# A fused attention and feed-forward kernel: transposes of the next chunk moved two pairs later, six q/k products gathered at the phase change, output products spread 2, 4, 5, 5

## The chip, the cores and the metric

The kernel runs on one core of one Trainium2 chip. The metric is the device time of one execution in microseconds (us), the median of several runs. The profile comes from one further execution of the same program, and its times are counted from that execution's first instruction.

## What is computed

The input x has 2048 rows of 448 numbers in bfloat16. Each row is normalized. From the normalized rows come a sliding-window attention (16 heads of width 28, each row attends to itself and the 7 rows at distances 2, 4, ..., 14 before it) and a feed-forward of width 1792. The output joins the two:

```python
xn = _layernorm(x)
qkv = xn @ wqkv                                   # 16 heads of 28
idx = pos[:, None] - (arange(8) * 2)[None, :]     # dilated window
attn = softmax(where(idx >= 0, einsum(q, k[idx]) * 28 ** -0.5, -1e9))
s = einsum(attn, v[idx]) @ wo
h = gelu(xn @ w1 + b1)
g = silu(h @ w2 + b2)
out = x + s * g
```

## The kernel before

Even rows are processed before odd rows, so that the dilated window is a plain one. The 2048 rows are 16 tiles of 128 rows, in four chunks of four tiles. Everything is kept in SBUF.

**Order of the work.** The instructions of TensorE (PE), ScalarE (ACT), VectorE (DVE) and GpSimd stand on each engine in the order in which the code issues them (`tc.manual_schedule`, L382). Instructions issued before L382 (memsets, DMAs) are placed by the scheduler.

**Start (L383 to L428).** Eight dummy matmuls (`busy`), then for tiles 0 to 3: statistics (`ln_stats`), the reciprocal deviation on ACT (`ln_rstd`), the normalization on DVE (`ln_apply`), four 128x128 transposes on PE (`ln_tr`) and a copy into the transposed array xnT (`ln_put`). Between them stand the first v products (`v_mm`). Then DVE spreads the q/k weights from the staging tile wraw to wqk (L182), and PE makes the q and k products of chunk 0. In this document T2 and T3 are the transposes of tiles 2 and 3, v1, v2, v3 the v products that follow.

**Four rounds, c = 0 to 3.** Each has two phases.

- `feed_forward_1(c)`: seven pairs k = 0 to 6 of first feed-forward products for chunk c. A pair is two PSUM banks, six full matmuls (L224) and two half-height ones (L233), and its two gelu activations on ACT (L239). `ffn1_even` ends with the half-height ones, `ffn1_odd` begins with them. Pair 0 is made in the phase before. Between the pairs stand: the transposes of chunk c+1 (after k = 1 and k = 3), two q and two k products of chunk c+1 (after k = 5), the silu of chunk c-1 (tanh on ACT, L268, then g on DVE, L269), the row statistics of chunk c+2, and output products (`wo_job`: four matmuls L288, then sg and o_t on DVE, then a DMA out on SP's queue).
- The attention phase (c below 3): the q and k products of head group 2, then five units of 121 queries. A unit is S (16 small matmuls, L312), two exp on ACT (L317), two mask products on DVE (L319), AV (16 small matmuls into psO, L328), a shuffle of the denominators on DVE (L332), Ln and Exp on ACT (L335, L336) and the division into oT on DVE (L337). Beside each unit stands one second feed-forward product (`ffn2_job`, 14 matmuls L257, called y0 to y15 here, put into SBUF by DVE at L264). The fifth unit is followed by pair 0 of the next chunk.

**The tail.** Before `feed_forward_1(3)` all but the last two units are done. After it stand units 15 and 16, y12 to y15, and the output products 8 to 15 (wo8 to wo15).

**PSUM.** Eight banks in two pools. psA (tag A) has two buffers of two banks, used by S and by the pairs k = 1, 2, 4, 5. psB (tag B) has four buffers of one bank, used by all else: pT, q/k, v, y, wo, psO and the pairs k = 0, 3, 6. A new psB tile gets the buffer that is released first in the order of the code, and its first matmul waits for the last reader of the tile before it. So a transpose can wait for a division of an attention unit, and a feed-forward pair for the sg of an output product.

**Waits through SBUF.** wraw has 904 columns. The DMAs write columns 0 to 895, and a memset (L125) clears columns 896 to 903; the ranges interleave row by row, and the memset waits for both DMAs.

Of the kernel before, what the change touches and what calls it, by code (L numbers as in the profile page):

```python
# [10 lines left out]
U32 = mybir.dt.uint32  # L11
# [22 lines left out]
def kernel(  # L34
# [60 lines left out]

    nc.vector.memset(wz[:].bitcast(U32), 0)
# [28 lines left out]
    nc.vector.memset(wraw[:, :, 2 * D:2 * D + 8].bitcast(U32), 0)  # L125
# [49 lines left out]
    def ln_put(t, pT, copy):  # L175
        copy(xnT[:, :, LEAD + t * P:LEAD + (t + 1) * P], pT[:, :, :])  # L176
# [16 lines left out]
    def q_job(c, g):  # L193
        qk_job(c, g, 0, nc.vector.tensor_copy)
# [19 lines left out]
    def ffn1_tiles(k):  # L214
        if k % 3 == 0:
            return [psB.tile([P, CH], F32, name="ps_h", tag="B") for _ in range(2)]
        ps = psA.tile([P, 2, CH], F32, name="ps_h", tag="A")
        return [ps[:, i, :] for i in range(2)]
# [130 lines left out]
    def feed_forward_1(c, ps, wos):  # L349
# [4 lines left out]
        for k in range(0, MT // 2, 2):  # L354
# [6 lines left out]
            if c + 1 < NC and k < 4:  # L361
                for j in (k, k + 1):
                    ln_put(nx + j, ln_tr(nx + j), nc.vector.tensor_copy)
            if c and k < 4:
                silu_job(4 * (c - 1) + k)
                silu_job(4 * (c - 1) + k + 1)
            if c + 1 < NC and k == 4:
                for g in range(2):
                    q_job(c + 1, g)
                    k_job(c + 1, g, nc.vector.tensor_copy)  # L370
            if c + 2 < NC and 2 <= k < 6:
                ln_stats(nx + 4 + k - 2)
                ln_stats(nx + 4 + k - 1)
            for _ in range(2):
                if k >= 2 and wos:
                    wo_job(wos.pop(0))
# [5 lines left out]
    with tc.manual_schedule(engines={ENG.PE, ENG.Activation, ENG.DVE, ENG.Pool}):  # L382
# [47 lines left out]
        for c in range(3):  # L430
            feed_forward_1(c, ps, [0, 1, 2] if c == 2 else [])
# [6 lines left out]
            q_job(n, 2)  # L438
            k_job(n, 2)
# [18 lines left out]
        feed_forward_1(3, ps, [3, 4, 5, 6, 7])  # L458
        wo_job(8)
        E = qk_unit(15)  # L460
        ffn2_job(12)
        s9 = wo_mm(9)
        norm = av_unit(15, E)
        wo_put(9, s9)
        E = qk_unit(16)
        norm()
# [3 lines left out]
        s10 = wo_mm(10)  # L470
        norm = av_unit(16, E)
        norm()
        wo_put(10, s10)
        nc.scalar.preload_act_table_set(SET_GELU)
        s11 = wo_mm(11)
        y14 = ffn2_job(14, False)
        wo_put(11, s11)
        s12 = wo_mm(12)
        ffn2_put(14, y14)
        wo_put(12, s12)  # L480
        silu_job(13)
        silu_job(14)
        s13 = wo_mm(13)
        wo_put(13, s13)
# [36 lines left out]
```

## Time and profile before

| | |
|---|---|
| median of 3 runs | 184.22 us (183.9 to 184.52) |
| the profiled execution | 184.21 us, of which the span from first to last instruction is 182.6 us |
| PE busy | 165.5 us (91%) |
| ACT busy | 125.3 us (69%) |
| DVE busy | 118.0 us (65%) |
| TensorE clock, mean granted | 0.972 of full speed |
| output DMAs | 16 of 112.0 KB, on SP's queue |

A row of the time order reads: start, duration, engine, line, operation, output<-input, shape, xcount, and in square brackets how long the engine was idle before it and what ended that. Rows merge equal instructions that follow each other; the duration then runs from the first start to the last end. Matmuls overlap, so what a stretch costs on PE is read from start to start. Some matmul records are missing, so a count may be one short.

The first feed-forward phase of chunk 1 lies at 61 to 79 us, that of chunk 2 at 100 to 121 us, that of chunk 3 at 143 to 159 us.

### The profile page before, as it was taken

The numbers are of one execution on the slowest core, as the hardware profiler recorded it, in microseconds if no ns is written. First come the engines' busy times: TensorE is split into PE (matmuls) and PEld (weight loads), VectorE is DVE, ScalarE is ACT, GpSimd is POOL, SyncE is SP. The second block draws the span as 40 slices with busy tenths as digits, with TensorE's granted clock in tenths as the row PEclk, the third lists the DMA queues.
The fourth block names the chain that finished last, engine by engine and source line by source line (L and its number), as shares of the span: only waits on it lengthen the run. The fifth ranks groups of instructions, "written<-read, shape, count | busy, mean of one in ns | idle before, by whom it ended". The sixth has DMA issues, their size and how long they took to land.

```text
span 182.6 us, 3260 instructions
## 1 busy us (share of the span) xinstructions
PE 165.5 (91%) x1308; PEld 76.6 (42%) x1324; DVE 118.0 (65%) x266; ACT 125.3 (69%) x197; POOL 4.6 (2%) x16
## 2 busy tenths in 40 slices
PE   7489999999999789999999679999999999999870
PEld 2144444444555334444544334445455343355430
DVE  6563864456888436938886546728676425977793
ACT  3633297466888699396879796186788699767620
POOL 6020000000000000000000000000000000000000
PEclk9958999999999999999999999999999999999996
DMA  5999951000000000000000000000000000210021
GB/s 153 220 284 317 377 148 40 0 0 5 0 4 0 0 0 4 0 0 0 4 0 4 2 0 25 25 29 0 4 0 0 4 2 0 101 54 25 25 75 50
DMA packets 10990, 9.03 MB, mean 49 GB/s; under 512 B 2592, under 2 KB 10976, under 8 KB 10976
## 3 DMA queue, kind: packets, MB, share of 16 engines
q1 hardware_dynamic: 10688, 8.61, 15.8%
q10 hardware_dynamic: 288, 0.23, 0.4%
q8 instruction: 10, 0.16, 0.4%
q14 instruction: 4, 0.03, 0.1%
HBM read 7.00 MB, written 1.84 MB: 48 GB/s over the span
## 4 chain that ended last, share of the span: by engine, by line
PE 60%; ACT 24%; DVE 8%; DMA 3%; issue 2%; SPq 1%; DVEq 0%
PE ps_y L257 18%; PE ps_qk L188 12%; PE ps_h L224 11%; ACT E L317 6%; PE ps_v L203 5%; ACT hT L239 5%; PE ps_s L288 4%; DMA wraw<-in_A_wqkv_dram 3%; PE S L312 3%; ACT den L336 3%; PE ps_h L233 3%; ACT den L335 2%; PE psO L328 2%; DVE sg L294 2%; DVE g L269 2%
## 5 line engine op out<-in xcount | busy, mean ns | idle before, releaser
L239 ACT ACTIVATE hT<-ps_h,b1f 128x512 bf16<-128x512 f32 x56 | 34.4, 701 | 15.7 <-PE ps_h L233 14.9
L257 PE MATMUL ps_y<-w,hT 128*128 128x448 bf16 x224 | 45.1, 353 | 0.0
L224 PE MATMUL ps_h<-xnT,w 128*128 128x512 bf16 x160 | 40.4, 380 | 0.6 <-DVE sg L294 0.2
L317 ACT ACTIVATE E<-S 128x976 bf16<-128x976 f32 x34 | 32.0, 986 | 7.3 <-PE S L312 6.3
L188 PE MATMUL ps_qk<-xnT,wqk 128*128 128x512 bf16 x120 | 29.2, 379 | 0.4
L257 PEld LDWEIGHTS <-hT 128*128 128x128 bf16 x224 | 20.8, 98 | 19.3
L319 DVE TENSOR_TENSOR E<-E,mk_gen 128x976 bf16<-128x976 bf16 x30 | 19.8, 665 | 10.8 <-ACT E L317 10.8
L224 PEld LDWEIGHTS <-w 128*128 128x128 bf16 x168 | 15.2, 98 | 20.1 <-issue 4.8
L337 DVE TENSOR_TENSOR oT<-psO,den 128x484 bf16<-128x484 f32 (+1 forms) x17 | 11.2, 661 | 12.4 <-ACT den L336 12.4
L188 PEld LDWEIGHTS <-wqk 128*128 128x128 bf16 x128 | 12.3, 98 | 14.9 <-issue 1.1
L191 DVE CAST qT<-ps_qk 128x512 bf16<-128x512 f32 x16 | 11.0, 687 | 10.4 <-PE ps_qk L188 10.4
L269 DVE SCALAR_TENSOR_TENSOR g<-th,y 128x448 bf16<-128x448 bf16 x15 | 8.7, 621 | 13.7 <-ACT th L268 13.7
L203 PE MATMUL ps_v<-wv,xnT 128*128 128x448 bf16 x68 | 17.2, 392 | 0.0
L288 PE MATMUL ps_s<-wo,oT 128*128 128x448 bf16 x64 | 13.9, 353 | 1.5 <-DVE xnT L176 1.0
L335 ACT ACTIVATE den<-den 128x484 f32<-128x484 f32 (+1 forms) x17 | 10.4, 611 | 5.3 <-DVE den L332 5.3
L208 ACT CAST vw<-ps_v 128x448 bf16<-128x448 f32 x17 | 9.1, 536 | 6.0 <-PE ps_v L203 6.0
L172 PE MATMUL pT<-ident,xnb 128*128 128x128 bf16 x64 | 6.1, 232 | 6.9 <-DVE oT L337 3.4
L332 DVE STREAM_SHUFFLE den<-psO 128x484 f32<-128x484 f32 (+1 forms) x17 | 11.8, 695 | 0.0
L268 ACT ACTIVATE th<-y 128x448 bf16<-128x448 f32 x15 | 8.2, 601 | 4.3 <-DVE y L264 4.3
L336 ACT ACTIVATE den<-den 128x484 f32<-128x484 f32 (+1 forms) x17 | 10.3, 605 | 0.5
L233 PE MATMUL ps_h<-xnT,w 64*128 64x512 bf16 x56 | 9.9, 383 | 0.5 <-ACT hT L239 0.2
L294 DVE SCALAR_TENSOR_TENSOR sg<-ps_s,g 128x448 bf16<-128x448 f32 x16 | 9.9, 616 | 0.2
(60 smaller groups left out, 132.1 us busy)
## 6 DMA issues: line engine op xcount, KB each, us to landing
out_dram<-o_t SPq DMA_DIRECT2D x16, 112.0 KB
w<-in_B_w_dram SPq DMA_DIRECT2D x1, 1568.0 KB
w<-in_B_w_dram SPq DMA_DIRECT2D x2, 672.0 KB
x<-in_A_x_dram SPq DMA_DIRECT2D x3, 448.0 KB
wraw<-in_A_wqkv_dram SPq DMA_DIRECT2D x1, 672.0 KB
w<-in_B_w_dram SPq DMA_DIRECT2D x4, 112.0 KB
wo<-in_A_wo_dram SPq DMA_DIRECT2D x16, 24.5 KB
wv<-in_A_wqkv_dram SPq DMA_DIRECT2D x1, 336.0 KB
```

The source lines that it names most:

```text
L188: nc.tensor.matmul(ps[:, :], wqk[:, kt, 16 * which + 4 * g:16 * which + 4 * g + 4, :], xnT[:, kt, LEAD + c * CH:LEAD + (c + 1) * CH], star ...
L203: nc.tensor.matmul(ps[:, :], xnT[:, kt, o:o + P], wv[:, kt, :], start=(kt == 0), stop=(kt == KT - 1))
L224: nc.tensor.matmul(ps[i][:, :], w1[:, kt, m * P:(m + 1) * P], xnT[:, kt, LEAD + c * CH:LEAD + (c + 1) * CH], start=(first and kt == 0), st ...
L233: nc.tensor.matmul(ps[i][:, :], w1[r, 3, m * P:(m + 1) * P], xnT[r, 3, LEAD + c * CH:LEAD + (c + 1) * CH], start=first, stop=not first)
L239: nc.scalar.activation(hT[:, m, :], ps[i][:, :], ACT.Gelu_apprx_tanh, bias=b1f[:, m:m + 1])
L257: nc.tensor.matmul(ps[:, :], hT[:, m, tt * P:(tt + 1) * P], w2[:, m, :], start=(m == 0), stop=(m == MT - 1))
L288: nc.tensor.matmul(ps[:, :], oT[:, g, t * P:(t + 1) * P], wo[:, g, :], start=(g == 0), stop=(g == 3))
L294: nc.vector.scalar_tensor_tensor(out=sg[:], in0=ps[:, :], scalar=0.5, in1=g_sb[t % NG][:], op0=ALU.mult, op1=ALU.mult)
L317: nc.scalar.activation(ev, Sp[p2][:, :, :, 0:QW], ACT.Exp, scale=SCALE)
L319: nc.vector.tensor_tensor(out=ev, in0=ev, in1=mkb, op=ALU.mult)
L335: nc.scalar.activation(den[:, :, 0:n], den[:, :, 0:n], ACT.Ln)
L336: nc.scalar.activation(den[:, :, 0:n], den[:, :, 0:n], ACT.Exp, scale=-1.0)
```

## The change

- The memset of wraw's last columns is issued first, ahead of the DMAs into wraw.
- Pair k = 6 gets a psA buffer instead of two psB buffers.
- In `feed_forward_1` the transposes of chunk c+1 stand after k = 3 and k = 5, no longer after k = 1 and k = 3. The silu of chunk c-1 stands there too. The statistics of chunk c+2 stand after k = 1 and k = 3.
- The q and k products of groups 0, 1 and 2 of the next chunk stand together after pair 6, all six copied out by DVE. Before, group 2 alone stood there and its k was copied by ACT.
- The output products per round are 0, 2, 4, 5 and 5 after the last round, where they were 0, 0, 3, 5 and 8. In rounds 1 and 2 they start at k = 4, in round 3 at k = 2.
- The tail is reordered: y12 stands before unit 15, wo8 to wo10 are gone from it, the silu of tile 13 uses the exp table (`silu_exp_job`), and unit 16's division comes after wo13's matmuls.

```diff
+    nc.vector.memset(wraw[:, :, 2 * D:2 * D + 8].bitcast(U32), 0)
     nc.vector.memset(wz[:].bitcast(U32), 0)
...
-    nc.vector.memset(wraw[:, :, 2 * D:2 * D + 8].bitcast(U32), 0)
...
-        if k % 3 == 0:
+        if k in (0, 3):
             return [psB.tile([P, CH], F32, name="ps_h", tag="B") for _ in range(2)]
...
-            if c + 1 < NC and k < 4:
-                for j in (k, k + 1):
-                    ln_put(nx + j, ln_tr(nx + j), nc.vector.tensor_copy)
-            if c and k < 4:
-                silu_job(4 * (c - 1) + k)
-                silu_job(4 * (c - 1) + k + 1)
-            if c + 1 < NC and k == 4:
-                for g in range(2):
-                    q_job(c + 1, g)
-                    k_job(c + 1, g, nc.vector.tensor_copy)
-            if c + 2 < NC and 2 <= k < 6:
-                ln_stats(nx + 4 + k - 2)
-                ln_stats(nx + 4 + k - 1)
+            if c + 2 < NC and k < 4:
+                ln_stats(nx + 4 + k)
+                ln_stats(nx + 5 + k)
+            if k in (2, 4):
+                if c + 1 < NC:
+                    for j in (k - 2, k - 1):
+                        ln_put(nx + j, ln_tr(nx + j), nc.vector.tensor_copy)
+                if c:
+                    silu_job(4 * (c - 1) + k - 2)
+                    silu_job(4 * (c - 1) + k - 1)
             for _ in range(2):
-                if k >= 2 and wos:
+                if k >= (2 if c == 3 else 4) and wos:
                     wo_job(wos.pop(0))
...
-            feed_forward_1(c, ps, [0, 1, 2] if c == 2 else [])
+            feed_forward_1(c, ps, [[], [0, 1], [2, 3, 4, 5]][c])
...
-            q_job(n, 2)
-            k_job(n, 2)
+            for g in range(3):
+                q_job(n, g)
+                k_job(n, g, nc.vector.tensor_copy)
...
-        feed_forward_1(3, ps, [3, 4, 5, 6, 7])
-        wo_job(8)
+        feed_forward_1(3, ps, [6, 7, 8, 9, 10])
+        ffn2_job(12)
         E = qk_unit(15)
-        ffn2_job(12)
-        s9 = wo_mm(9)
-        norm = av_unit(15, E)
-        wo_put(9, s9)
-        E = qk_unit(16)
-        norm()
         g12 = silu_exp_job(12)
         ffn2_job(13)
         g12()
-        s10 = wo_mm(10)
+        s11 = wo_mm(11)
+        norm = av_unit(15, E)
+        wo_put(11, s11)
+        E = qk_unit(16)
+        g13 = silu_exp_job(13)
+        norm()
+        y14 = ffn2_job(14, False)
+        s12 = wo_mm(12)
         norm = av_unit(16, E)
-        norm()
-        wo_put(10, s10)
-        nc.scalar.preload_act_table_set(SET_GELU)
-        s11 = wo_mm(11)
-        y14 = ffn2_job(14, False)
-        wo_put(11, s11)
-        s12 = wo_mm(12)
+        g13()
         ffn2_put(14, y14)
         wo_put(12, s12)
-        silu_job(13)
+        s13 = wo_mm(13)
+        norm()
+        nc.scalar.preload_act_table_set(SET_GELU)
+        wo_put(13, s13)
         silu_job(14)
-        s13 = wo_mm(13)
-        wo_put(13, s13)
         y15 = ffn2_job(15, False)
```

At the start, on DVE, these are the instructions around the normalization of tile 2 (xnb_76), with a minus what stood there only before:

```order
 L156 BN_STATS st<-x_70 128x6
 L157 BN_AGGR mv<-st 128x2
-L125 MEMSET wraw 128x4x4
 L164 TENSOR_SCALAR xnb_76<-x_70,mv,rstd 128x448
 L167 COPY xnb_76<-xnb_76 128x64
```

The memset that waits for wraw's DMAs is gone from between the statistics of tile 3 and the normalization of tile 2; it is DVE's first memset now.

In the feed-forward phase of chunk 1, ACT had this order before (den is the last division's Ln and Exp, th the tanh of the silu):

```order
L336 ACTIVATE den<-den 128x484
L351 ACT_TABLE_LOAD
L239 ACTIVATE hT<-ps_h,b1f 128x512 x4
L268 ACTIVATE th<-y 128x448 x2
L239 ACTIVATE hT<-ps_h,b1f 128x512 x4
L268 ACTIVATE th<-y 128x448 x2
L239 ACTIVATE hT<-ps_h,b1f 128x512 x6
```

and has this one now:

```order
L336 ACTIVATE den<-den 128x484
L351 ACT_TABLE_LOAD
L239 ACTIVATE hT<-ps_h,b1f 128x512 x8
L268 ACTIVATE th<-y 128x448 x2
L239 ACTIVATE hT<-ps_h,b1f 128x512 x4
L268 ACTIVATE th<-y 128x448 x2
L239 ACTIVATE hT<-ps_h,b1f 128x512 x2
```

The first two tanh stand behind the gelu of four pairs instead of two. On PE the transposes move with them, so that pairs 1, 2 and 3 now follow the last AV without a transpose between.

In the tail, from unit 15's exp on, ACT had this order before (se is the silu by exp, den the denominators of units 15 and 16):

```order
L317 ACTIVATE E<-S 128x8x122 x4
L335 ACTIVATE den<-den 128x484
L336 ACTIVATE den<-den 128x484
L275 ACTIVATE se<-y 128x448
L276 ACTIVATE se<-se 128x448
L277 ACTIVATE se<-se 128x448
L335 ACTIVATE den<-den 128x4x112
L336 ACTIVATE den<-den 128x4x112
```

and has this one now:

```order
L317 ACTIVATE E<-S 128x8x122 x2
L275 ACTIVATE se<-y 128x448
L276 ACTIVATE se<-se 128x448
L277 ACTIVATE se<-se 128x448
L317 ACTIVATE E<-S 128x8x122 x2
L275 ACTIVATE se<-y 128x448
L276 ACTIVATE se<-se 128x448
L277 ACTIVATE se<-se 128x448
L335 ACTIVATE den<-den 128x484
L336 ACTIVATE den<-den 128x484
```

Two silu chains instead of one now stand ahead of unit 15's Ln and Exp.

## The prediction

> **What bounds the kernel now.** I read the page first, then the time order of PE, the waits, and the time order of ACT and DVE around each gap of PE.
>
> ```profile
> PE 165.5 (91%) x1308; PEld 76.6 (42%) x1324; DVE 118.0 (65%) x266; ACT 125.3 (69%) x197; POOL 4.6 (2%) x16
> ```
>
> PE is busy for 91% of the span and no PE work is removed, so the change can only win where PE waits or runs slowly. The first such place is the start (stretches of the start with the granted clock in the third column from the right, then PE's time order):
>
> ```profile
> 8.00:8.50 0.50, 0.00 (x0) 0.00 (x0) 0.00 (x0) 0.47 (x2) 0.00 (x0) 0.85 0.25 19
> ...
> 15.00:15.50 0.50, 0.50 (x4) 0.18 (x3) 0.00 (x0) 0.09 (x1) 0.00 (x0) 0.82 1.05 387
> ```
>
> ```profile
> 1.26 3.60 PE L347 MATMUL ps_w<-wz 128*128 128x512 bf16 x8 [1.26 <-DVE wz L96]
> ...
> 9.93 0.61 PE L172 MATMUL pT<-ident,xnb 128*128 128x128 bf16 x4 [2.17 <-DVE xnb L164]
> ...
> 12.25 3.13 PE L203 MATMUL ps_v<-wv,xnT 128*128 128x448 bf16 x8
> 15.21 7.07 PE L188 MATMUL ps_qk<-xnT,wqk 128*128 128x512 bf16 x31
> ```
>
> PE waits 2.17 us for T2's input, and the clock is at half from about 8.35 to about 15.2 us (0.85 and 0.82 are mixtures of 1.0 and 0.5). What holds T2's input is on DVE:
>
> ```profile
> 7.28 0.18 DVE L157 BATCH_NORM_AGGREGATE mv<-st 128x2 f32<-128x6 f32 x1
> 9.47 0.07 DVE L125 MEMSET wraw<- 128x16 uint32 x1 [2.01 <-DMA wraw<-in_A_wqkv_dram]
> 9.47 0.40 DVE L164 TENSOR_SCALAR xnb<-x,mv,rstd 128x448 bf16<-128x448 bf16 x1
> ```
>
> A memset of 0.07 us stands in DVE's queue and waits for a DMA that T2 doesn't need.
>
> The second place is the feed-forward phase of chunk 1 (PE, then ACT), with the same picture in chunk 2:
>
> ```profile
> 62.52 0.39 PE L172 MATMUL pT<-ident,xnb 128*128 128x128 bf16 x4
> 64.63 0.40 PE L172 MATMUL pT<-ident,xnb 128*128 128x128 bf16 x4 [1.73 <-DVE oT L337]
> 64.87 1.46 PE L224 MATMUL ps_h<-xnT,w 128*128 128x512 bf16 x6
> ...
> 68.10 0.61 PE L172 MATMUL pT<-ident,xnb 128*128 128x128 bf16 x8
> 68.55 1.46 PE L224 MATMUL ps_h<-xnT,w 128*128 128x512 bf16 x6
> ```
>
> ```profile
> 65.19 2.42 ACT L239 ACTIVATE hT<-ps_h,b1f 128x512 bf16<-128x512 f32 x4
> ```
>
> The second transpose waits for the division of the last attention unit, whose psB buffer it takes. Two tiles' transposes cost 0.45 us from start to start (68.10 to 68.55); here they cost 2.35 (62.52 to 64.87), so 1.90 us is lost. Two pairs cost 3.23 (64.87 to 68.10).
>
> **The change part by part.** All sums are made against the profiled execution, 184.21 us with a span of 182.6; the median of the runs is 184.22, so the two are one number here.
>
> *The memset.* L164 can start when the aggregate at 7.28 ends, 7.46, and T2 follows 0.46 later (9.47 to 9.93 now): 7.92. From T2 to the end of T3 takes 2.32 us at half clock (9.93 to 12.25), so v2 would start at 10.24; v2 and v3 take 2.96 (12.25 to 15.21). If the clock stays low as long after T2 as now, the whole piece only moves by 2.0. If it returns earlier, more. The eight dummy matmuls took 0.45 us each, double the 0.22 of the q/k products at 15.21 (31 in 7.07), so the clock was low until about 4.9 too. Changes at 4.9, 8.35 and 15.2 are 3.45 and 6.85 apart, once and twice the same step; by that PE's unbroken work from 7.9 on would bring the clock back at 8.35 + 3.4 = 11.75. Then v2 and v3 are at half clock for 1.51 of their 2.96 us and need 0.73 for the rest, and the q products start at 12.48 instead of 15.21. Bounds: 2.0, and about 4.6 if the clock never falls (half of the 5.28 from T2 to q: 7.92 + 2.64 = 10.56). I take **-2.7**, since the step accounts for three changes. The weight copies (L182) still wait for wraw and still end before q needs them; the DMA of wraw gains a wait for a memset that ends long before SP reaches it, which costs nothing.
>
> [...]
>
> *The phase change.* In chunks 0 and 1 the first AV of a phase waits:
>
> ```profile
> 43.65 0.23 PE L328 MATMUL psO<-E,vw 128*32 128x122 bf16 x2
> ...
> 44.40 0.40 PE L312 MATMUL S<-qT,kT 28*128 28x122 bf16 x16
> ```
>
> ```profile
> PE psO L328 <- DVE E L319: 0.4, 2, 0.2
> ```
>
> AV takes 0.75 from start to start there and 0.34 later (162.53 to 162.87, below). Six q/k products (24 matmuls of 0.23 by the row at 15.21, 5.5 us) give ACT time to finish gelu, table load and deviations ahead of S, and the k copy leaves ACT. So both waits go: **-0.8**. DVE takes that copy too; the cover is PE's own time for the products, and without it the first mask product, and with it AV, would be late by one copy.
>
> *Transposes two pairs later, chunks 1 and 2.* The 1.90 goes in each. Two waits take its place. Pair 2 ends at 62.52 + 1.6 = 64.1, and pair 3 now takes the division's buffer, free at 64.6: 0.5. Pair 3 ends at 64.63 + 1.6 = 66.2, transposes 66.7, and pair 4 needs pair 1's buffer, which ACT frees with the fourth gelu at 65.19 + 2.42 = 67.6: 0.95. Nothing but 0.45 us of transposes covers that any more. Chunk 1: -1.90 + 0.5 + 0.95 = **-0.45**. In chunk 2 another wait goes:
>
> ```profile
> 108.73 1.68 PE L288 MATMUL ps_s<-wo,oT 128*128 128x448 bf16 x8 [0.95 <-DVE xnT L176]
> 110.25 1.46 PE L224 MATMUL ps_h<-xnT,w 128*128 128x512 bf16 x6
> ```
>
> Output products waited for transposes' buffers, behind g in DVE's queue; now their buffers come from gelu, done earlier. Chunk 2: -0.45 - 0.95 = **-1.4**. An output product costs 0.76 (1.52 for two); 16 stay 16, so their new places sum to nothing. Queued behind DVE's sg, the first q products could wait up to 0.3 in chunk 2; I take 0. The earlier statistics on DVE lie beside pairs 2 and 3, ahead of copies that PE needs only at the q products.
>
> *Chunk 3.*
>
> ```profile
> 149.64 1.46 PE L224 MATMUL ps_h<-xnT,w 128*128 128x512 bf16 x5
> ...
> 153.25 1.68 PE L288 MATMUL ps_s<-wo,oT 128*128 128x448 bf16 x8
> 154.97 0.81 PE L224 MATMUL ps_h<-xnT,w 128*128 128x512 bf16 x3
> 155.93 0.81 PE L224 MATMUL ps_h<-xnT,w 128*128 128x512 bf16 x3 [0.15 <-DVE sg L294]
> ...
> 156.99 1.77 PE L288 MATMUL ps_s<-wo,oT 128*128 128x448 bf16 x8
> 158.69 0.40 PE L312 MATMUL S<-qT,kT 28*128 28x122 bf16 x16
> ```
>
> ```profile
> PEld L233 <- DVE oT L337: 0.6, 1, 0.6
> ```
>
> Two pairs take 3.61 (149.64 to 153.25) instead of 3.23, two output products 1.72 and 1.70 instead of 1.52, and pair 6 waits 0.15 for sg. With gelu ahead of tanh and pair 6 in psA all four go: **-0.9**. The wait of pair 3 for the division, 0.6 here, stays; it is the model for the 0.5 above.
>
> *The tail.* From unit 15 on:
>
> ```profile
> 162.53 0.40 PE L328 MATMUL psO<-E,vw 128*32 128x122 bf16 x16
> 162.87 0.40 PE L312 MATMUL S<-qT,kT 28*128 28x122 bf16 x16
> 163.19 2.82 PE L257 MATMUL ps_y<-w,hT 128*128 128x448 bf16 x14
> 165.85 0.92 PE L288 MATMUL ps_s<-wo,oT 128*128 128x448 bf16 x4
> ...
> 175.34 1.68 PE L288 MATMUL ps_s<-wo,oT 128*128 128x448 bf16 x8
> ```
>
> ```profile
> 163.29 1.86 ACT L317 ACTIVATE E<-S 128x976 bf16<-128x976 f32 x2 [1.77 <-PE S L312]
> 165.04 0.61 ACT L335 ACTIVATE den<-den 128x484 f32<-128x484 f32 x1
> ...
> 166.19 0.56 ACT L275 ACTIVATE se<-y 128x448 f32<-128x448 f32 x1
> ```
>
> ```profile
> 168.00 0.63 DVE L280 SCALAR_TENSOR_TENSOR g<-se,y 128x448 bf16<-128x448 f32 x1 [0.49 <-ACT se L277]
> ...
> 168.55 0.67 DVE L332 STREAM_SHUFFLE den<-psO 128x448 f32<-128x448 f32 x1
> ...
> 176.46 0.62 DVE L264 TENSOR_TENSOR y<-ps_y,b2bc 128x448 f32<-128x448 f32 x1
> ...
> 179.33 0.39 DVE L297 TENSOR_TENSOR o_t<-x,sg 128x448 bf16<-128x448 bf16 x1
> ```
>
> Let unit 16's S start at s. PE then has S 0.32, y14 2.66, wo12 0.76 and AV 0.34, and reaches wo13 at s + 4.08. wo13's buffer was unit 15's psO, so it waits for that division. Ahead of it on ACT stand two exp (from s + 0.42, 1.75), three silu steps (0.6 each with the gap, 1.8) and Ln and Exp (1.25), then about 0.65 on DVE for the division (the shuffle of the same tile takes 0.67): s + 5.87. PE waits 1.8. y15's buffer is freed by y14's put, three DVE operations of about 0.58 after the division: s + 7.65, when wo13 ended at s + 6.68, another 0.95. y15 ends at s + 10.3; DVE then needs about 0.2 and the 3.26 from 176.46 to 179.72: s + 13.8. S of unit 15 begins 4.08 before s, so the tail takes 17.9 from there. It takes 21.03 now (158.69 to 179.72), of which two output products move away: 19.5 against 17.9, but y12's 2.66 now stands in front, 20.5 against 19.5: **+1.0**.
>
> Sum: -2.7 - 0.8 - 0.45 - 1.4 - 0.9 + 1.0 = -5.25, and 184.2 - 5.3 = **178.9 us**. A measurement of this kernel can tell about 0.3%, 0.55 us, from no change.
>
> **The rivals.**
>
> 1. *The clock returns late at the start.* The step may be chance. At half clock until 15.2, q starts at 13.2 and 2.0 us of q work pass at half speed, 1.0 lost: the term is -1.0, and the time 180.6. [...]
> 2. *The clock doesn't fall at the start.* T2 follows v0 closely: -4.6, and 177.0. [...]
> 3. *The clock falls in the tail.* 1.8 and 0.95 us of waiting lie within 3.7 us. One step of 3.4 at half clock costs 1.7: 180.6. The 1.73 at 64.63 did not do it; this is more.
> 4. *The waits only move.* If chunks 1 to 3 win nothing (-0.45, -1.4 and -0.9 fall away): 181.7.
> 5. *Slower.* The clock falls at each new group of waits. Chunks 1 and 2 have 1.45 us of idling within one step, the tail 2.75; at half clock each costs 1.7, 5.1 in all, and with the first rival's 1.7 the time is 185.7. It decides from the point at which 1.45 idle of 3.4 lowers the clock; 1.73 did not at 64.63, so the chance is small.
>
> That the change doesn't do what it says is no rival: the memset's place and the later transposes stand in the order.
>
> **How the numbers follow.** Forecast 57%, first rival 14%, second 10%, third 11%, fourth 6%, fifth 2%. The forecast's own range, from the small unknowns (0.3 in chunk 2, half of each tail wait), is 178.0 to 179.9. The range reaches to rivals 1 to 3: 176.9 to 180.9. Only the fifth is not faster by 0.3%; with something unseen I give faster 0.96, same 0.02, slower 0.02.
>
> **What would show it.** In the changed profile T2 starts near 7.9 with no L125 behind a DMA, and q near 12.5; the clock is at 0.5 for one step. No transpose waits for a division; pair 3 does for about 0.5 and pair 4 for gelu about 0.95 in chunks 1 and 2. No first AV waits. wo13 waits 1.8 for a division, y15 0.95 for DVE's put. I am wrong if q starts after 13.5, if the clock falls after 20 us, or if the transposes still wait.

## The result and the profile after

The changed kernel takes **177.91 us** (median of 4 runs, 177.48 to 178.78) where the kernel before takes 184.19 (4 runs, 183.9 to 184.52): a ratio of 0.9664, 95% interval 0.9624 to 0.9705, or 6.2 us less. The forecast was 178.9 with a range from 176.9 to 180.9. Single slow runs, more than 1.5% above the fastest of their kernel, are left out of every ratio in this document. The profiled execution took 178.06 us with a span of 176.4. The page of the changed kernel, its busy time and its clock row:

```profile
PE 163.9 (93%) x1324; PEld 75.6 (43%) x1324; DVE 120.0 (68%) x269; ACT 124.7 (71%) x196; POOL 4.5 (3%) x16
...
PEclk9999999999999999999999999999999999999998
```

PE has no less work. Its share rises because idle time goes, and no slice shows a lower clock until after PE's last matmul. Stages are cut at the first row of a kind in PE's time order (first feed-forward pair, S of a unit, end of the last o_t on DVE). Work that only moves from one stage to another, an output product at 0.76 us and y12 at 2.75, is taken out in the column "left":

| stage | before | after | difference | of which moved work | left | forecast |
|---|---|---|---|---|---|---|
| start to the first feed-forward pair | 22.12 | 18.62 | -3.50 | | **-3.50** | -2.7 |
| first pair to the first S of chunk 0's round | 17.59 | 17.60 | +0.01 | | 0 | 0 |
| first to second S, chunks 0 and 1 | 4.69 + 4.69 | 4.27 + 4.28 | -0.83 | | **-0.83** | -0.8 |
| last S of chunk 0's round to the first of chunk 1's | 21.78 | 22.85 | +1.07 | +1.52 | **-0.45** | -0.45 |
| last S of chunk 1's round to the first of chunk 2's | 25.15 | 24.37 | -0.78 | +0.76 | **-1.54** | -1.4 |
| last S of chunk 2's round to unit 15's S | 19.82 | 20.74 | +0.92 | +2.75 - 0.76 | **-1.07** | -0.9 |
| unit 15's S to the end of the last o_t | 21.03 | 17.99 | -3.04 | -2.75 - 1.52 | **+1.23** | +1.0 |

The column "left" sums to -6.16, and 184.21 less 178.06 is 6.15. All but the start came within 0.25 us of the forecast. The start of the changed kernel, PE's time order:

```profile
6.92 0.92 PE L203 MATMUL ps_v<-wv,xnT 128*128 128x448 bf16 x4
7.84 0.45 PE L172 MATMUL pT<-ident,xnb 128*128 128x128 bf16 x4
8.12 0.92 PE L203 MATMUL ps_v<-wv,xnT 128*128 128x448 bf16 x4
...
10.92 5.34 PE L188 MATMUL ps_qk<-xnT,wqk 128*128 128x512 bf16 x24
16.90 1.89 PE L188 MATMUL ps_qk<-xnT,wqk 128*128 128x512 bf16 x8 [0.64 <-DVE qT L191]
18.62 1.46 PE L224 MATMUL ps_h<-xnT,w 128*128 128x512 bf16 x6
```

T2 starts at 7.84 (7.92 expected) and q at 10.92, where the forecast had 12.48: v1 runs its four matmuls in 0.92 us, at full clock. But PE then waits 0.64 at a q product, which nothing in the forecast named. DVE's time order tells why:

```profile
7.42 0.36 DVE L164 TENSOR_SCALAR xnb<-x,mv,rstd 128x448 bf16<-128x448 bf16 x1
...
9.75 1.75 DVE L182 COPY wqk<-wraw 128x512 bf16<-128x512 bf16 x8 [1.01 <-DMA wraw<-in_A_wqkv_dram]
...
15.43 0.63 DVE L156 BATCH_NORM_STATS2 st<-x 128x6 f32<-128x448 bf16 x1 [2.75 <-DMA x<-in_A_x_dram]
...
16.19 0.66 DVE L191 CAST qT<-ps_qk 128x512 bf16<-128x512 f32 x1
```

It is the picture of the memset again, one place further in the queue: DVE now arrives before the DMA of x's tiles 4 to 7 has landed, stands at their statistics for 2.75 us, and the q casts that free PE's buffers stand behind. Of the 4.29 us won up to q (15.21 to 10.92), 0.8 is given back.

At the phase change of chunk 0 the first AV no longer waits: it takes 0.33 us from start to start, where it took 0.75.

```profile
40.16 0.40 PE L328 MATMUL psO<-E,vw 128*32 128x122 bf16 x16
40.49 0.40 PE L312 MATMUL S<-qT,kT 28*128 28x122 bf16 x16
```

Chunk 1's feed-forward phase on PE, with the waits of the weight loads below:

```profile
60.00 1.11 PE L233 MATMUL ps_h<-xnT,w 64*128 64x512 bf16 x4
...
62.35 0.63 PE L172 MATMUL pT<-ident,xnb 128*128 128x128 bf16 x8
63.75 1.46 PE L224 MATMUL ps_h<-xnT,w 128*128 128x512 bf16 x6 [0.77 <-ACT hT L239]
```

```profile
PEld L233 <- DVE oT L337: 1.8, 3, 0.6
```

The transposes no longer wait, pair 3 waits 0.6 for the division (its half-height matmuls take 1.11 instead of 0.61), and pair 4 waits 0.77 for gelu. The forecast had both waits at these places, with 0.5 and 0.95. The tail on PE:

```profile
155.56 0.40 PE L312 MATMUL S<-qT,kT 28*128 28x122 bf16 x16
...
165.58 0.93 PE L288 MATMUL ps_s<-wo,oT 128*128 128x448 bf16 x4 [1.62 <-DVE oT L337]
167.21 2.81 PE L257 MATMUL ps_y<-w,hT 128*128 128x448 bf16 x14 [0.69 <-DVE y L264]
```

wo13 waits 1.62 (1.8 expected) and y15 0.69 (0.95 expected).

### The profile page after: what moved, and what is told of

Same layout as the page of the kernel before. It is cut to its first block, busy times and chain, and to the rows that moved or that the text cites. A ratio compares the mean times of both kernels' runs of the same rounds, so it can differ in the third digit from the quotient of the medians.

```text
span 176.4 us, 3278 instructions
## 1 busy us (share of the span) xinstructions
PE 163.9 (93%) x1324; PEld 75.6 (43%) x1324; DVE 120.0 (68%) x269; ACT 124.7 (71%) x196; POOL 4.5 (3%) x16
## 3 DMA queue, kind: packets, MB, share of 16 engines
HBM read 7.00 MB, written 1.84 MB: 50 GB/s over the span
## 4 chain that ended last, share of the span: by engine, by line
PE 68%; ACT 15%; DVE 7%; SPq 4%; DMA 3%; issue 2%; DVEq 0%
PE ps_y L257 23%; PE ps_h L224 13%; PE ps_qk L188 13%; PE ps_s L288 6%; ACT E L317 4%; PE S L312 3%; PE ps_v L203 3%; DMA x<-in_A_x_dram 3%; PE ps_h L233 3%; ACT hT L239 3%; ACT den L336 2%; PE psO L328 2%; SPq L106 2%; ACT den L335 2%; DVE den L332 2%
## 5 line engine op out<-in xcount | busy, mean ns | idle before, releaser
L239 ACT ACTIVATE hT<-ps_h,b1f 128x512 bf16<-128x512 f32 x56 | 33.9, 708 | 2.6 <-PE ps_h L233 2.2
L269 DVE SCALAR_TENSOR_TENSOR g<-th,y 128x448 bf16<-128x448 bf16 x14 | 8.2, 621 | 14.1 <-ACT th L268 14.1
L203 PE MATMUL ps_v<-wv,xnT 128*128 128x448 bf16 x68 | 15.2, 353 | 0.1
L335 ACT ACTIVATE den<-den 128x484 f32<-128x484 f32 (+1 forms) x17 | 10.4, 610 | 5.4 <-DVE den L332 5.4
L156 DVE BATCH_NORM_STATS2 st<-x 128x6 f32<-128x448 bf16 x16 | 9.8, 610 | 5.0 <-DMA x<-in_A_x_dram 5.0
L233 PE MATMUL ps_h<-xnT,w 64*128 64x512 bf16 x56 | 10.5, 384 | 0.4
L264 DVE TENSOR_TENSOR y<-ps_y,b2bc 128x448 f32<-128x448 f32 x16 | 9.9, 618 | 0.9 <-PE ps_y L257 0.8
```

Of the source, the lines that this page charges most:

```text
L203: nc.tensor.matmul(ps[:, :], xnT[:, kt, o:o + P], wv[:, kt, :], start=(kt == 0), stop=(kt == KT - 1))
L233: nc.tensor.matmul(ps[i][:, :], w1[r, 3, m * P:(m + 1) * P], xnT[r, 3, LEAD + c * CH:LEAD + (c + 1) * CH], start=first, stop=not first)
L239: nc.scalar.activation(hT[:, m, :], ps[i][:, :], ACT.Gelu_apprx_tanh, bias=b1f[:, m:m + 1])
L335: nc.scalar.activation(den[:, :, 0:n], den[:, :, 0:n], ACT.Ln)
```

## The experiments

All are compared with the kernel before in the same session; its medians there were 184.53, 184.78 and 184.65 us. Where a stage is named, it comes from the run's profile.

### The start

**The memset back at its old place**, the rest of the change kept.

```diff
-    nc.vector.memset(wraw[:, :, 2 * D:2 * D + 8].bitcast(U32), 0)
     nc.vector.memset(wz[:].bitcast(U32), 0)
...
+    nc.vector.memset(wraw[:, :, 2 * D:2 * D + 8].bitcast(U32), 0)
```

> The changed kernel with one line undone: the memset of wraw's last columns stands again behind the DMAs into wraw, as in the kernel before. Theory (the start term is -3.5 us, because with an early T2 the clock does not fall at all): T2 back at about 9.9 us, the granted clock at 0.5 from about 8.35 to 15.2, the first feed-forward pair back from 18.62 to about 22.1, all later stages as in the changed kernel: 177.9 + 3.5 = 181.4 us. First rival (the fall of the clock belongs to this place and only one step of it was saved, the forecast's own case): the part is worth 2.7, 180.6 us. Second rival (something else in the change, not the memset, keeps the clock up): T2 late by 2.0 but the clock at 1.0 throughout, 177.9 + about 1.2 = 179.1 us, since the DMA of x that DVE waits for later hides some of the 2.0.

Measured: 182.44 us, ratio 0.9898 (0.9852 to 0.9945). PE's time order of this kernel:

```profile
10.45 0.45 PE L172 MATMUL pT<-ident,xnb 128*128 128x128 bf16 x4 [2.76 <-DVE xnb L164]
10.73 1.65 PE L203 MATMUL ps_v<-wv,xnT 128*128 128x448 bf16 x4
...
14.90 7.07 PE L188 MATMUL ps_qk<-xnT,wqk 128*128 128x512 bf16 x31
21.81 1.46 PE L224 MATMUL ps_h<-xnT,w 128*128 128x512 bf16 x6
```

The first pair is back at 21.81, every later stage equals the changed kernel's within 0.02 us, and the profiled 181.25 is 178.06 + 3.19. It is the fastest of the four runs; the median lies 1.0 above the 181.4 expected, and why is open. The theory's mechanism holds, with the clock at half for 3.41 us (10.77 to 14.18), not 6.85, and T2 later than expected (10.45). The second rival falls: without the early memset the clock does drop.

**The memset alone**, in the kernel before (the same lines the other way).

> The kernel before with one line of the change alone: the memset of wraw's last columns issued first. Theory (the part stands on its own and is the largest term: T2 early and the clock not falling; the profile of the changed kernel gives 3.5 us from the start to the first feed-forward pair): T2 at about 7.9 us, granted clock 1.0 throughout, first feed-forward pair at 18.0 to 18.6 instead of 22.1, and later stages as before, 184.2 - 3.5 = 180.7 us. Rival (the forecast's case, one step of 3.4 us at half clock stays): 184.2 - 2.7 = 181.5 us. Second rival (what is won at the start is lost in chunk 0, since the gelu of pair 0 stands on ACT behind the deviations of tiles 4 to 7, which come with the DMA of x): first pair at 18, but chunk 0 longer by up to 0.9, 181.6 us.

Measured: 180.41 us, ratio 0.9775 (0.974 to 0.9809), about 4.1 us less by the ratio. First pair at 18.02, no low clock, later stages as before within 0.02 us (chunk 0 17.59: nothing is lost there). The two ratios multiply to 0.9675, the whole change's: the memset and the rest add up. By the ratios the memset alone is about two thirds of the gain.

**The memset back, and PE kept busy** by ten dummy matmuls while T2's input is late.

```diff
         v_put(0, v0)
+        busy(10)
         ln_apply(2)
```

> The changed kernel with the memset back at its old place, behind the DMAs into wraw, and with ten dummy matmuls on PE in the idle time ahead of T2's transposes (v0's end to T2). T2 is late as in the kernel before, but PE doesn't idle before it. Theory (what T2's lateness costs and what the clock costs are two things, and the fall of the clock comes from PE's idle time): granted clock 1.0 throughout the start, T2 at 9.9 to 10.5 us, and from T2 to the first feed-forward pair the same 10.1 us at full clock as with an early T2 and no wait for q: first pair at 20.0 to 20.6 us, where it is 21.81 with the memset back and no dummies; time about 179.8 us. Rival (the fall comes with T2's late start or the load of the DMAs, not from idling): clock falls to 0.5 for one or two steps of 3.4 us all the same, first pair at 21.8 or later, 181.3 us or more.

Measured: 181.88 us, ratio 0.983 (0.9791 to 0.987). PE's time order:

```profile
6.93 1.70 PE L203 MATMUL ps_v<-wv,xnT 128*128 128x448 bf16 x4
8.42 3.29 PE L347 MATMUL ps_w<-wz 128*128 128x512 bf16 x10
11.55 0.39 PE L172 MATMUL pT<-ident,xnb 128*128 128x128 bf16 x4
...
21.48 1.46 PE L224 MATMUL ps_h<-xnT,w 128*128 128x512 bf16 x6
```

T2 to the first pair takes 9.93 us (10.1 expected), so from T2 on PE is at full clock, though T2 and wraw's DMA are late: the rival falls. That PE's idling makes the clock fall is not shown by it. The clock's column has 1.00 in the whole start, but by its durations PE ran at half speed up to about 10.4: v0 took 1.70 us instead of 0.92, and about half of the dummies were slow (3.29 us for ten, 0.33 each between 0.45 and 0.22). So there was no full clock to lose in this run while T2 was late; that PE's unbroken work ahead of T2 brought it up is not shown. A run at full clock with a late T2 and a busy PE is missing. The time and T2's place were missed too: wraw's DMA was late (the memset at 10.36) and the slow dummies lasted longer, so that T2 started at 11.55. The profiled run, at 183.35 the longest of four, lost 0.83 and 1.62 more in chunk 2 and the tail, both told below.

So the start parts into two costs. From T2 to the first pair it takes 9.93 us at full clock without a wait, 11.36 with the clock at half for 3.41 us (memset back), 12.19 with 6.83 us of it (before: 9.93 to 22.12; 11.65 in the second profile below, where T2 came later). In the profile of before the lateness of T2 (9.93 instead of 7.84) cost 2.1 us and the clock 2.3; the changed kernel wins both and gives 0.8 back at the q casts.

**Both kernels once more**, unchanged, for a second profile.

> The kernel before, unchanged, for a second profile of its start. Theory (the step of the granted clock stands at a phase that is free of the kernel's start: 8.35 to 15.2 in the first profile, 10.9 to 14.3 in the changed kernel with the memset back): the clock falls once in the 8 to 16 us stretch, for one or two steps of about 3.4 us, at another place than 8.35; T2 between 9.5 and 10.6 by the DMA of wraw; first feed-forward pair between 21 and 22.5; stages after it equal to the first profile within 0.1 us each. Rival (the fall is tied to PE's idling there): at 8.35 again for 6.85 us.

Measured: 184.47 us. T2 at 10.70, first pair at 22.35, later stages equal within 0.02 us; the clock is low from 8.02 to 14.85, 6.83 us again. T2 is 0.10 later than expected. This run alone doesn't tell the two apart (8.02 is not 8.35, but near), and what sets the place of the fall is not shown; where the clock changed in the other profiles stands in the last section.

> The changed kernel, unchanged, for a second profile. Theory (its stages are fixed, and what differs between runs is the start, by the DMAs of wraw and x, and whether one step of the clock falls in the tail, as it did for 3.4 us with the transposes back and with the dummies): first feed-forward pair between 17.7 and 18.7, stages up to unit 15 equal within 0.1 us, and from unit 15 to the end either 17.99 or about 19.65. Rival (the tail's clock holds in this kernel): 17.99 again.

Measured: 178.26 us. First pair at 18.83, 0.13 above the expected range, since the wait for the q cast was 0.96 this time; the tail is 17.99 again.

**The statistics behind the q casts**, and **x's DMA earlier**.

```diff
             if g == 3:
-                ln_stats(7)
+                for t in range(4, 8):
+                    ln_stats(t)
                 ln_rstd(4, 4)
-            else:
-                ln_stats(4 + g)
```

> The changed kernel with the four row statistics of tiles 4 to 7 moved behind the last q cast of the start; nothing else. In the changed kernel DVE's statistics of tile 4 wait 2.75 us for the DMA of x, the q casts stand behind it, and PE waits 0.64 us for a q buffer. Theory: that wait is the whole cost and goes: first feed-forward pair at about 18.0 instead of 18.62, time 177.9 - 0.64 = 177.3 us. Rival (the wait is covered by what follows: the statistics then delay the k copies, the deviations on ACT or the first gelu, and PE waits there instead): 177.9 us, no change.

Measured: 178.69 us, ratio 0.9696 (0.9647 to 0.9746): nothing won. PE, then ACT:

```profile
17.78 1.46 PE L224 MATMUL ps_h<-xnT,w 128*128 128x512 bf16 x6
...
25.56 1.46 PE L224 MATMUL ps_h<-xnT,w 128*128 128x512 bf16 x6 [0.71 <-ACT hT L239]
```

```profile
20.77 0.30 ACT L160 ACTIVATE lnv<-mv,eps_t 128x4 f32<-128x4 f32 x1 [3.94 <-DVE mv L157]
...
23.09 7.17 ACT L239 ACTIVATE hT<-ps_h,b1f 128x512 bf16<-128x512 f32 x12
```

The first pair is 0.84 earlier, and chunk 0's feed-forward takes 18.46 instead of 17.60: 0.86 given back. The theory falls, the rival holds. On ACT the deviations, the table load and gelu stand behind the last statistics, so gelu 0 moves from 22.61 to 23.09, while the first pair is earlier, and PE runs into it.

```diff
+    nc.sync.dma_start(x_sb[1][:, :, :], dram_rows(x_par, 4, 4))
     nc.sync.dma_start(b1t[:], B_b1.rearrange("(m f) -> f m", f=P))
...
-        if c0 == 0:
-            nc.sync.dma_start(x_sb[1][:, :, :], dram_rows(x_par, 4, 4))
```

> The changed kernel with the DMA of x's tiles 4 to 7 issued ahead of the first half of w1 instead of behind it. In the profile of the changed kernel DVE's statistics of tile 4 wait 2.75 us for that DMA, q casts stand behind them, and ACT's deviations with gelu 0 behind those. Moving the statistics away from the casts won 0.84 us to the first pair and lost 0.86 again in chunk 0, where pair 3 waited 0.71 for gelu. Theory (the DMA itself is the cause, for the casts and for gelu): no wait at q, first pair at about 17.8, and chunk 0 stays at 17.60: 177.9 - 0.7 = 177.2 us, with less spread between runs. Rival (w1's first half now lands too late: PE waits for it at the first pair): first pair later than 18.6, 178.5 us or more.

Measured: 177.61 us (median of five runs, 177.2 to 178.93; a sixth, left out, took 180.33), ratio 0.9627 (0.959 to 0.9665). In the profile the mechanism is as expected: no wait at q, first pair at 17.74, gelu 0 at 20.87 instead of 22.61, chunk 0 at 17.59, span 175.5 instead of 176.4. But the runs spread no less than before, and the intervals overlap: a gain is not shown.

Other profiles say why. Six have the changed kernel's own start, and in them tile 4's statistics, which wait for x's DMA, begin at 14.38, 14.60, 14.88, 15.29, 15.43 and 15.63. From q to the first pair these take 6.91, 7.04, 7.37, 7.60, 7.70 and 8.03 us, in the same order, where 6.91 is the time without a wait. So x's DMA is the cause, but when it lands early by itself, the first pair is at 17.69 with its issue at the old place.

### Chunks 1 to 3

**The transposes back behind pairs 1 and 3.**

```diff
+            if c + 1 < NC and k < 4:
+                for j in (k, k + 1):
+                    ln_put(nx + j, ln_tr(nx + j), nc.vector.tensor_copy)
             if c + 2 < NC and k < 4:
...
             if k in (2, 4):
-                if c + 1 < NC:
-                    for j in (k - 2, k - 1):
-                        ln_put(nx + j, ln_tr(nx + j), nc.vector.tensor_copy)
```

> The changed kernel with only the transposes of the next chunk put back behind pairs 1 and 3; the silu, the statistics, the output products and pair 6's buffer stay where the change put them. Theory (the waits do not only move, they are smaller at the new place): in chunks 1 and 2 the second transpose waits again for the division, about 1.9 us, and the 0.6 for pair 3 and the 0.77 for pair 4 go, so each chunk is about 0.4 us longer (between 0.35 and 0.53): 177.9 + 0.8 = 178.7 us. Chunk 0 has no division ahead of it and stays. Rival (waits only move, their sum is set by the attention unit's end on DVE and ACT): 177.9 us. Second rival: without the silu between, the transposes' copies queue differently on DVE and both kinds of wait stand: 179.9 us.

Measured: 180.09 us, ratio 0.9754 (0.9713 to 0.9794). PE in chunk 1 and in the tail:

```profile
60.17 0.40 PE L172 MATMUL pT<-ident,xnb 128*128 128x128 bf16 x4 [1.73 <-DVE oT L337]
...
167.54 4.49 PE L257 MATMUL ps_y<-w,hT 128*128 128x448 bf16 x14 [0.69 <-DVE y L264]
```

The stages of chunks 1 and 2 are 23.29 and 24.81 instead of 22.85 and 24.37: +0.44 each, inside the theory's 0.35 to 0.53; chunk 0 stays at 17.60. The waits shrink at the new place and don't only move. The start was 0.55 shorter than in the changed kernel's profile (first pair at 18.07). The other 1.7 us of this run are in a place that the edit doesn't touch: y15's matmuls take 4.49 us instead of 2.81, and unit 15's S to the end 19.68 instead of 17.99. Stretches of this kernel's tail, clock in the third column from the right:

```profile
164.57:167.99 3.42, 1.38 (x7) 0.67 (x8) 2.80 (x6) 2.05 (x4) 0.00 (x0) 1.00 0.00 0
167.99:171.40 3.41, 3.41 (x11) 1.39 (x10) 2.41 (x6) 1.56 (x2) 0.00 (x0) 0.50 0.20 67
```

That is the forecast's third rival, the clock that falls in the tail, with its price (1.7 there, 1.69 here). It happened in this profile and in that of the dummies (19.61), and in neither profile of the changed kernel. That the changed kernel's slowest run (178.78, mean clock 0.988 where the others have 0.997 to 0.999) was one of these is likely and not shown, as it has no trace.

**The q and k products of groups 0 and 1 back ahead of pair 6.**

```diff
+            if c + 1 < NC and k == 4:
+                for g in range(2):
+                    q_job(c + 1, g)
+                    k_job(c + 1, g, nc.vector.tensor_copy)
...
-            for g in range(3):
-                q_job(n, g)
-                k_job(n, g, nc.vector.tensor_copy)
+            q_job(n, 2)
+            k_job(n, 2, nc.vector.tensor_copy)
```

> The changed kernel with the q and k products of groups 0 and 1 back ahead of pair 6 (behind the transposes and output products that stand there now); group 2 stays behind pair 6, and its k copy stays on DVE. It tells apart the two things to which the forecast gave the first AV's wait. Theory (the six products' time is what covers ACT): pair 6's gelu, the table load and the deviations again end behind the first S, and the first AV of chunks 0 and 1 waits about 0.4 us each: from S to S 4.69 instead of 4.27, together +0.84. Rival (the k copy, 0.46 us from start to start on ACT right ahead of the first exp, was the whole of it): 4.27 to 4.35 from S to S, no loss there. By either, chunk 0 may lose 0.2 to 0.6 us as q's products now stand right behind the second pair of transposes and wait for their copies. Time 177.9 + 0.84 to 1.4 by the theory, 177.9 + 0.2 to 0.6 by the rival.

Measured: 179.83 and 180.57 us (182.58 and 182.63 are left out); two runs are too few for a ratio. The profiled 180.57 is 2.5 above the changed kernel's 178.06, and its stages account for that. PE around the phase change of chunk 0 and ahead of that of chunk 1:

```profile
29.86 3.61 PE L188 MATMUL ps_qk<-xnT,wqk 128*128 128x512 bf16 x16 [0.62 <-DVE xnT L176]
...
36.86 0.39 PE L312 MATMUL S<-qT,kT 28*128 28x122 bf16 x16
...
41.13 0.40 PE L312 MATMUL S<-qT,kT 28*128 28x122 bf16 x16
...
72.14 1.99 PE L188 MATMUL ps_qk<-xnT,wqk 128*128 128x512 bf16 x8 [0.66 <-DVE sg L294]
```

From S to S it is 4.27 us in chunks 0 and 1: the rival holds. The four products moved away had no part in the first AV's wait. What is left of the change at this place is the k copy and pair 6's buffer. So the k copy's leaving ACT is the likely cause of the whole; a run with that copy alone back on ACT is missing. What they are for shows elsewhere: chunk 0's feed-forward takes 18.38 instead of 17.60, and chunks 1 and 2 take 23.78 and 25.29 instead of 22.85 and 24.37. Ahead of pair 6 the products wait for the transposes' copies (chunk 0) and for sg of the output products (chunks 1 and 2), 0.62 to 0.67 each time. These waits are what the later transposes and output products would have cost there.

### The tail

**Unit 15's division ahead of tile 13's silu, y14's put ahead of tile 13's g.**

```diff
         E = qk_unit(16)
-        g13 = silu_exp_job(13)
         norm()
+        g13 = silu_exp_job(13)
         y14 = ffn2_job(14, False)
         s12 = wo_mm(12)
         norm = av_unit(16, E)
-        g13()
         ffn2_put(14, y14)
+        g13()
```

> The changed kernel with two steps of the tail's order moved: unit 15's division (its Ln and Exp on ACT with it) stands ahead of tile 13's silu, and y14's put ahead of tile 13's g. Theory (the tail's 1.62 us wait of output product 13 is made by the three silu steps on ACT that stand ahead of Ln and Exp, and the 0.69 of y15 by the operations ahead of the put): output product 13 starts at about 163.9 instead of 165.58, y15 at about 165.4 instead of 167.2, and the end moves by 1.85: 176.1 us. Rival (the tail's end is set by the chain of ACT and DVE, silu of tiles 13, 14 and 15 one behind the other, and PE has slack): PE's waits go but the end moves by less than 0.6: 177.3 to 177.9 us.

Measured: **176.2 us, ratio 0.9545 (0.9508 to 0.9583)**. PE's tail:

```profile
154.75 0.40 PE L312 MATMUL S<-qT,kT 28*128 28x122 bf16 x16
...
163.09 0.93 PE L288 MATMUL ps_s<-wo,oT 128*128 128x448 bf16 x4
164.44 2.81 PE L257 MATMUL ps_y<-w,hT 128*128 128x448 bf16 x14 [0.42 <-DVE y L264]
```

The wait of wo13 is gone, that of y15 is 0.42, and unit 15's S to the end takes 16.34 us instead of 17.99: 1.65 of the 1.85 expected. The interval lies below that of the changed kernel, so this version beats both.

**The same with y14's put ahead of unit 16's shuffle, and with x's DMA earlier.**

```diff
-        norm = av_unit(16, E)
         ffn2_put(14, y14)
+        norm = av_unit(16, E)
```

> The changed kernel with three moves: x's tiles 4 to 7 ahead of w1's first half in the DMA queue; in the tail unit 15's division ahead of tile 13's silu (as in the run before, 16.34 us from unit 15 to the end where the changed kernel takes 17.99); and y14's put ahead of unit 16's shuffle on DVE. Theory: start -0.8 against the changed kernel's profile, tail -1.65, and the last wait of y15 (0.42 us) goes as well: 178.06 - 2.9 = 175.2 us. Rival for the last part (unit 16's division, delayed by the put's 0.6 us, then holds output product 13's reader or DVE's last chain): no gain from it, 175.6 us.

Measured: 176.53 us, ratio 0.9547 (0.9515 to 0.9578): the same as without. y15 no longer waits, and the tail takes 16.37 us. Chunk 0 takes 17.89 instead of 17.60, as the first q product behind pair 6 waited 0.23 for a transpose's copy in this profile. PE is no longer what sets the end. DVE's time order (its lines are one lower in this kernel), then that of the run without this move:

```profile
167.49 0.63 DVE L268 SCALAR_TENSOR_TENSOR g<-th,y 128x448 bf16<-128x448 bf16 x1 [0.17 <-ACT th L267]
168.03 0.62 DVE L263 TENSOR_TENSOR y<-ps_y,b2bc 128x448 f32<-128x448 f32 x1
```

```profile
167.82 0.62 DVE L264 TENSOR_TENSOR y<-ps_y,b2bc 128x448 f32<-128x448 f32 x1
```

Taken from each kernel's S of unit 15 (154.93 and 154.75), y15's put stands at 13.10 and 13.07: DVE's chain, with tile 14's silu ahead of it, is as late as before, and the rival holds in that nothing is won.

**Output products of chunks 1 and 2 from pair 3 on**, with the tail of the first of these two.

```diff
-                if k >= (2 if c == 3 else 4) and wos:
+                if k >= 2 and wos:
```

> The changed kernel with unit 15's division and y14's put moved forward as in the earlier run of that tail, and with the output products of chunks 1 and 2 starting behind pair 3's transposes (two there in each chunk, the other two of chunk 2 behind pair 5) instead of behind pair 5. Theory (pair 4 waits 0.77 us for gelu, and output products that stand ahead of it cover that): about 0.4 to 0.77 us less in each of chunks 1 and 2, as output products may wait up to 0.4 for the transposes' buffers: 22.1 to 22.45 instead of 22.85 from the last S of chunk 0's round to the first of chunk 1's, 23.6 to 24.0 instead of 24.36 in the next; 176.2 - 1.0 = 175.2 us. Rival (the wait only moves: the output products wait for the transposes' copies on DVE as in the kernel before, 0.95, or q's products then wait for sg behind g): no gain, 176.2 us or up to 0.5 more.

Measured: 176.58 us, ratio 0.9568 (0.9522 to 0.9614): the same. PE in chunks 1 and 2:

```profile
63.02 1.68 PE L288 MATMUL ps_s<-wo,oT 128*128 128x448 bf16 x8 [0.98 <-DVE xnT L176]
...
102.25 1.67 PE L288 MATMUL ps_s<-wo,oT 128*128 128x448 bf16 x8 [0.27 <-DVE xnT L176]
```

Chunk 2 wins 0.48 (23.88), chunk 1 loses 0.20 (23.05). In chunk 1 the statistics of the last four tiles stand on DVE ahead of the transposes' copies, up to 62.58; in chunk 2 none do, and the copies start at 101.77, as soon as PE has made the transposes (begun at 101.34). So the same move wins in one and loses in the other.

## Why the prediction was right, and where not

- *The memset, -2.7.* This is the term that was mis-sized: -3.50 in the profile, -4.10 with the memset alone. The step that failed is the clock. The forecast kept its fall at 8.35 and let "PE's unbroken work from 7.9 on" end it one step later. The clock doesn't fall at all: its column has 1.00 through the start of the changed kernel and of the kernel with the memset alone. In the 3.41 us ahead of 8.35 PE is busy for 1.65 us in the kernel before, and for 2.27 at the same place with the memset alone (rows in the last section); that the early T2 kept the clock up by this work is not shown. That was rival 2 of the forecast, with a tenth of the chance.
- *What the forecast left out at the start* is what DVE meets next in its queue: the DMA of x, 0.8 us back. The two misses have opposite signs, q 1.56 us earlier than forecast and 0.79 lost behind it, so that the total came nearer than its parts is in part luck. There is a small slip too: T2 at 7.92 stands 0.43 ahead of the fall, and the sum ran it at half clock; by the forecast's own rule q would start at 12.26, not 12.48. The sentence that the weight copies "still end before q needs them" held in so far as no q product waits for one; the last copy ends at 11.50, behind the first q product at 10.92.
- *The phase change, -0.8.* Measured -0.83, for another reason than the main one given. The forecast put the six products first; the experiment leaves them no part, and the k copy's leaving ACT is what remains, though it wasn't tested alone. That DVE took the copy cost nothing.
- *The transposes two pairs later.* Right in size (-0.45 against -0.45, -1.54 against -1.4) and in its waits. The experiment gives +0.44 per chunk for undoing them. That the sum came out needed something that the forecast didn't name: with the products of two groups back ahead of pair 6, chunks 0 to 2 lose 0.78 to 0.93 each. So the later transposes and output products only work together with the products behind pair 6.
- *Chunk 3, -0.9.* Measured -1.07.
- *The tail, +1.0.* Measured +1.23, with the two waits at their places. That wo13 waits for the silu chain ahead of Ln and Exp on ACT was shown by moving tile 13's behind them.
- *The rivals.* The second happened, less what the DMA of x takes back. The first and the fifth did not occur in a profile. The fourth, that waits only move, fell. The third occurred in no profile of the changed kernel, but in two of its variants, with the price given.

What stays open: why runs of one kernel spread by 1 to 3 us. In the profiles with the changed kernel's own start the first pair varies by 1.1 us (17.69 to 18.83), which follows the landing of x's DMA, and the tail varies by 1.7 with the clock. In the profile with the dummies, DVE also waited for an output DMA in chunk 2 (1.08, row below), with four output products in that phase and three o_t buffers; PE waited 0.66 for a q cast behind it, and the stage took 25.19 instead of 24.37. How often that happens is not known.

```profile
118.00 0.39 DVE L297 TENSOR_TENSOR o_t<-x,sg 128x448 bf16<-128x448 bf16 x1 [1.08 <-DMA out_dram<-o_t]
```

## What to carry to other kernels

Here an instruction that waited for a DMA held what stood behind it on its engine: the memset of 0.07 us waited 2.01 us and held the normalization of tile 2; with that wait gone, tile 4's statistics waited 2.75 us and held a q cast. When one such wait is removed, look at once for the next DMA in the same queue, since the engine now gets there earlier. Price an edit near a fall of PE's clock twice, with the fall and without: here the changed kernel, with T2 at 7.84 instead of 9.93, had no fall in the start, where the clock had been at half for 6.83 us. A wait taken from PE is worth nothing where ACT or DVE carry the same delay to the next stage (with the statistics behind the q casts the first pair came 0.84 us earlier, and chunk 0 gave 0.86 back), so follow their queues to that stage before counting it.

## What the runs showed of the hardware

The granted clock was at 0.50 from 8.35 to 15.18 in the profile of the kernel before and from 8.02 to 14.85 in its second profile, 6.83 us each, and for 3.41 us from 10.77 to 14.18 with the memset back, from 167.99 to 171.40 with the transposes back and from 170.80 to 174.21 with the dummies. In the changed kernel's profile it fell at 175.19 only, behind PE's last matmul. The rows are single stretches of 3.41 us, counted off in that length from a change of the clock in the same profile; the number after the length is PE's busy time, and the clock is the third from the right. The rows come from the kernel before, the kernel before with the memset alone, the changed kernel, and the changed kernel with the memset back:

```profile
4.94:8.35 3.41, 1.65 (x12) 0.80 (x12) 2.38 (x9) 2.76 (x9) 0.00 (x0) 1.00 1.01 244
8.35:11.77 3.42, 1.84 (x8) 1.02 (x9) 2.23 (x12) 0.71 (x2) 0.00 (x0) 0.50 0.91 246
```

```profile
4.97:8.38 3.41, 2.27 (x18) 1.26 (x19) 3.12 (x11) 2.81 (x10) 0.00 (x0) 1.00 0.96 246
```

```profile
4.52:7.94 3.42, 2.04 (x15) 0.95 (x15) 3.22 (x12) 2.60 (x10) 0.00 (x0) 1.00 1.03 275
...
164.95:168.36 3.41, 2.08 (x11) 1.01 (x12) 3.38 (x8) 2.16 (x3) 0.00 (x0) 1.00 0.00 0
```

```profile
3.94:7.36 3.42, 1.85 (x15) 0.81 (x13) 3.21 (x12) 2.37 (x8) 0.00 (x0) 1.00 1.03 294
7.36:10.77 3.41, 0.65 (x7) 0.28 (x6) 0.77 (x5) 1.01 (x4) 0.00 (x0) 1.00 0.71 111
10.77:14.18 3.41, 3.41 (x15) 1.60 (x14) 2.06 (x11) 1.60 (x3) 1.10 (x4) 0.50 1.04 321
...
167.78:171.20 3.42, 1.74 (x9) 0.84 (x10) 3.12 (x7) 2.05 (x4) 0.00 (x0) 1.00 0.00 0
```

In the 3.41 us ahead of a fall PE was busy for 0.65 (memset back), 1.19 (dummies, 167.39 to 170.80), 1.38 (transposes back, above), 1.65 (before) and 1.83 us (second profile of before, 4.61 to 8.02). In other stretches of the rows it was busy for 1.74, 1.85, 2.04, 2.08 and 2.27, and the clock stayed at 1.00 behind them. The 1.83 lies among these, so PE's busy time alone doesn't part the two kinds, and what makes the clock fall is not shown. The fall at 8.35 came with PE idle for at most 0.80 us at a stretch in the 3.41 us ahead of it. From 8.35 to 11.77 PE was busy for 1.84 us and the clock stayed at 0.50; it came back at 15.18 behind 3.41 us of unbroken work, as at 14.18 with the memset back. The cleanest pair is the kernel before and the same with the memset alone: their stretches lie 0.03 us apart, T2 with the v product behind it makes 1.65 into 2.27, and the clock fell behind the first and held behind the second. In the changed kernel's profile T2 adds only 0.10 to the stretch that ends at 7.94. In the next one, 7.94 to 11.35, PE is busy for 3.28 us, where it was 0.65 in the stretch ahead of the fall (7.36 to 10.77) with the memset back. The same tail has 2.08 in one profile (164.95 to 168.36) and 1.38 in another (164.57 to 167.99), and the clock fell only behind the second.

The granted clock's column does not show the slow PE at the beginning of the run with ten dummies ahead of T2: v0 took 1.70 us for four matmuls at 6.93 with the column at 1.00, where it took 0.92 in the kernel before (at 6.84) and in the changed kernel (at 6.92). There PE stayed slow up to about 10.4, an estimate from the 3.29 us of the ten dummies.
